# First keys and queries in halves of 256 tokens in lent PSUM banks, with the scheduler's constants fitted anew

## Chip, cores and metric

One core of one Trainium2 chip. The metric is device time in microseconds (us) of that core; lower is better. A time quoted is the median of several executions. Profiles are of one execution each, so a single place in a profile can be off by what one execution differs from the next.

## The reference

One transformer block with layer norm ahead of attention and ahead of a gated feed-forward without a nonlinearity. 2048 tokens, model width 640, 32 heads of 20, feed-forward width 1728, all inputs bf16.

```python
h  = x + softmax(q @ k.T * 20 ** -0.5) @ v @ wo      # q, k, v = layernorm(x) @ wqkv, 32 heads of 20
h2 = h + ((ln(h) @ w_gate) * (ln(h) @ w_up)) @ w_down
```

There are 32 x 2048 x 2048 = 134 million exponentials. They set the pace: ScalarE, which takes 1738 of the 2048 blocks, is busy for 804.5 of the 860.7 us of the profile before the change.

## The kernel before

The kernel contains a scheduler that runs when the kernel is built. It holds an estimate of every instruction's duration, keeps a clock for each engine, and emits the instructions in the order in which its clocks say they would start. So a wrong estimate does no harm to the result, but it puts instructions in a wrong order, and that order is what the chip runs.

Scores are made in *bursts* into PSUM tiles `A` of two or three banks (1024 or 1536 columns). ScalarE takes the exponential of a burst; VectorE makes some blocks itself from banks of `m` or `A`, with integer arithmetic. Then the value product goes into bank `acc`. A *block* is 128 keys by 512 columns of scores; there are 2048 of them. Heads are handled in groups of four, tokens in chunks of 512. All other matmuls (projections, output, gate, up and down) are background *groups*, put in between bursts into the banks `m`. Where TensorE would be idle, *filler* is issued: matmuls on a zero tile `zt`.

```python
# Engines.run: what a transfer is believed to take
if e == "SP":
    self.ring = max(self.ring, s + t.dur) + t.size / 160.0
    slack = SLACK if t.prio > 0 else 300.0            # SLACK = 2000 ns
    t.ev.t = self.ring + 1500.0 + slack

# Pe.fill: what a group of four filler matmuls is believed to take
n = bank.shape[1]
self.charge(s, n / 2.4 + 3.0, self.shape(), float(n), deps, [])

# a background product: four matmuls of 32 columns, or one of 128 once attention is done (mode "F")
def columns(ps, lhsT, rhs, start, stop, n, width=P):
    if pe.mode == "F":
        mm(ps[0:width, 0:n], lhsT[:, 0:width], rhs, start, stop)
        return
    for i in range((width + 31) // 32):
        w = min(32, width - 32 * i)
        mm(ps[32 * i:32 * i + w, 0:n], lhsT[:, 32 * i:32 * i + w], rhs, start, stop)

# the opening: layer norm and transposes of 512 tokens, then keys (1) and queries (0) of two head groups
t0 = stage1_ln(0)
pe.groups += t0
pe.groups += [proj_direct(1, 0, 0, "ACT"), proj_direct(0, 0, 0, "ACT")]
pe.groups += [proj_direct(1, 1, 0, "ACT"), proj_direct(0, 1, 0, "DVE")]
... # cut: further chunks of 512 tokens, values, and the groups due later, with LEAD, LEADQ, LEADK
```

`proj_direct(b, g, ch)` makes five matmul steps over 512 tokens into one bank `m`, which ScalarE or VectorE then evacuates. It needs all four transposed tiles of 128 tokens.

The softmax here doesn't subtract the row's maximum and nothing guards it: scores larger than these inputs give would overflow.

Of the kernel before, what the change touches and what calls it, by code (L numbers as in the profile page):

```python
# [15 lines left out]
P = 128  # L16
# [39 lines left out]
class Ev:  # L56
# [3 lines left out]
    def __init__(self, t=None):  # L60
        self.t, self.slack = t, 0.0


class Max:
# [5 lines left out]
    @property  # L70
    def t(self):
        r = 0.0
        for e in self.es:
            if e.t is None:
                return None
            r = max(r, e.t)
        return r
# [116 lines left out]
class Pe:  # L194
# [78 lines left out]
    def next(self):  # L273
        s, kind, a, latest = self.choose()
        t = self.en.free["PE"]
        if self.att.flat == 0:
            t = max(t, known([self.zeros]))
        if t < INF and (kind == 2 or s > t + 100.0):
            if known([self.zeros]) <= t and (self.att.flat == 0 or sum(w for x, w in self.recent if x > t - TICK) < ENOUGH):
                need = FILL + SWITCH + (SWITCH if self.mode != self.shape() else 0.0)  # L280
                if t + need <= max(latest, s) + 20.0 and t < INF:
                    if self.att.summing() is not None or self.att.between(t) or not self.att.begun or any(b.free.t is not None and b.free.t <= t for b in self.mbanks):
                        return t + 10.0, self.fill
        return s, a

# [38 lines left out]
TICK = 3413.0  # L324
RWEIGHT = 128.0
FILL = 216.0
WINDOW = 30
EBUFS = (3, 5)
NED = 4
NI16 = 3  # L330
SLACK = 2000.0
THIRD = True
AHEAD = 9
VPARTS = [(0, 8), (8, 8), (16, 16)]
OPENS = 4
ENOUGH = 5000.0
SPREAD = (1.0, 1.0, 0.9, 0.8, .8)
LAG0 = 8
LEAD = 64
LEADQ = 64  # L340
LEADK = 16
M_END = 1800
BACK = 14

# [2 lines left out]
def kernel(  # L347
# [31 lines left out]
    def single_banks():  # L379

        if att.flat < att.total or att.a_free[0].t is None or att.a_free[1].t is None or att.third.t is None or len(pools) > 1:
            return
        pools[0].release()
        pools.append(tc.alloc_tile_pool(name="last", bufs=1, space=PSUM))
        for i, t in enumerate(tiles(pools[1], 5, [P, QW], F32, "b")):
            b = Bank(t[:])
            b.free = att.third if i == 2 else att.a_free[0] if i < 2 else att.a_free[1]
            pe.mbanks.append(b)
# [60 lines left out]
    def dve_ns(n, rate=1.0):  # L449
        return n / 0.96 / rate + 70.0  # L450
# [46 lines left out]
    class Att:  # L497
        def __init__(self):
# [47 lines left out]
            self.pending_act = 0.0  # L546
            self.q0 = [sum(WIDTHS[:i]) for i in range(len(WIDTHS))]
            self.kev = {}
            self.qev = {}
            self.vev = {}  # L550

# [93 lines left out]
        def inputs(self, b):  # L645
            s, j = b
            p, g, kg = self.slots[s]
            deps = [self.qev.get((g, p))]
            for k, _, _, _ in pieces(WIDTHS[p], kg):
                deps.append(self.kev.get((g, k // TPC)))  # L650
            return deps if all(d is not None for d in deps) else [Ev()]

        def summing(self):
# [238 lines left out]
    pe = Pe(en, att, filler)  # L892
    en.pe = pe
    def hook():
        single_banks()
        staged()
    en.hook = hook
    pe.mbanks = [Bank(m[:]) for m in mb]

    nn = [0]  # L900
    on_ev = {}
# [284 lines left out]
    def columns_of(b, ch):  # L1186

        return (att.q0[ch], WIDTHS[ch]) if b == 0 else (ch * QW, QW)
# [1 line left out]
    def tokens_ready(o, w):  # L1190
        return [Later(lambda tt=tt: lnT_ev.get(tt)) for tt in range(o // P, (o + w) // P)]

    def proj_direct(b, g, ch, eng="DVE"):
        t0, w = columns_of(b, ch)
        sl = slice(t0, t0 + w)
        o = b * D + g * HP * DH

        def step(c):
            def fn(ps, first, last):
                for j in range(HP):  # L1200
                    mm(ps[32 * j:32 * j + 32, 0:w], Wr[:, c, o + DH * j:o + DH * j + 32], lnT[:, c, sl], first, last)
            return fn

        def evac(ps, e):
            if b == 1:
                if eng == "ACT":
                    r = en.add("ACT", w / 1.2 + 63.0, [e], lambda: nc.scalar.copy(kT[g][:, sl], ps[:, 0:w]), 0)
                else:
                    r = en.add("DVE", dve_ns(w), [e], lambda: nc.vector.tensor_copy(kT[g][:, sl], ps[:, 0:w]), 0.8)
                att.kev[g, ch] = r  # L1210
            else:
                if eng == "ACT":
                    r = en.add("ACT", w / 1.2 + 63.0, [e], lambda: nc.scalar.mul(qT[ch][:, g, :], ps[:, 0:w], kap[:, 0:1]), 0)
                else:
                    r = en.add("DVE", dve_ns(w), [e], lambda: nc.vector.tensor_scalar_mul(qT[ch][:, g, :], ps[:, 0:w], kap[:, 0:1]), 0.8)
                att.qev[g, ch] = r
            return r
        ws = [e_qk0[b]]
        if b == 0:
            ws.append(e_kap)  # L1220
        return Group(tokens_ready(t0, w) + ws, [(pe_ns(w), step(c), []) for c in range(KC)], evac, f"P{b}{g}{ch}")
# [332 lines left out]

    t0 = stage1_ln(0)
    pe.groups += t0
    pe.groups += [proj_direct(1, 0, 0, "ACT"), proj_direct(0, 0, 0, "ACT")]
    pe.groups += [proj_direct(1, 1, 0, "ACT"), proj_direct(0, 1, 0, "DVE")]
    first = pe.groups[-3].ev

# [39 lines left out]

REPORT = []
D_GAP = 0
SHARE = 0.17
D_START = 2 * HP * NT
D_LAST = 40
D_LOAD = 4000.0
D_LOAD0 = 600.0
# [31 lines left out]
```

## Time and profile before

| | before |
|---|---|
| time | 863.93 us, median of 3 (862.95 to 864.56) |
| first exponential | 18.94 us |
| block 1920 of 2048 reaches an engine | 770.12 us |
| last score matmul | 825.61 us |
| end of the profiled execution | 860.67 us |

In this view of stretches each row has its bounds and its length, then the busy time and the number of instructions of TensorE (PE), its weight loads, VectorE, ScalarE (ACT) and GpSimd, the granted TensorE clock, the DMA share, and GB/s. The bounds are: first exponential, third head group (block 128), block 1920, last score, end.

```profile
0.00:18.94 18.94, 16.59 (x317) 8.22 (x317) 10.02 (x35) 4.74 (x7) 6.55 (x20) 1.00 0.81 241
18.94:85.44 66.50, 61.85 (x1365) 28.18 (x1364) 38.34 (x104) 58.91 (x52) 7.38 (x4) 1.00 0.21 57
85.44:770.12 684.68, 656.95 (x12076) 265.16 (x12076) 648.66 (x1321) 682.55 (x636) 6.29 (x7) 1.00 0.25 63
770.12:825.61 55.49, 54.04 (x1720) 34.61 (x1719) 40.08 (x99) 53.06 (x51) 0.69 (x1) 1.00 0.33 73
825.61:860.67 35.06, 31.22 (x381) 24.46 (x378) 17.34 (x49) 5.19 (x16) 0.55 (x1) 0.98 0.05 16
```

In the third row ScalarE is busy for 682.55 of 684.68 us: it is the bound.

### The profile page before, as it was taken

Reading aid. Unit: us, or ns where it says so; the run is one execution under the profiler, and the core shown is the slowest. Engines: PE = TensorE matmul, PEld = TensorE weight load, DVE = VectorE, ACT = ScalarE, POOL = GpSimd, SP = SyncE. Lnnn points to the kernel's source line nnn. Section 1 sums busy time; section 2 is a strip of 40 time slices with the busy share of each in tenths; the row PEclk is TensorE's granted clock in tenths of the full one; section 3 lists DMA queues with packets and bytes.
Section 4 is the critical chain, followed back from the end, with each engine's and each line's share of the span. In section 5 each row is a group of like instructions: output and inputs, shape, how many; then the busy total and the mean of one; then the engine's idle time right before and its main releaser. Section 6 shows DMA issues by size and latency. Waiting matters only on the chain. (4 is left out here: it accounts for less than half of the span.)

```text
span 860.7 us, 35389 instructions
## 1 busy us (share of the span) xinstructions
PE 820.7 (95%) x15853; PEld 360.6 (42%) x15853; DVE 754.4 (88%) x1607; ACT 804.5 (93%) x760; POOL 21.5 (2%) x33
## 2 busy tenths in 40 slices
PE   8899999999989999999989999999999999999998
PEld 4444333223423322223434433344444444556676
DVE  5664889999989999989989999999999999878663
ACT  3889999999999999999999999999999999999941
POOL 3020000000000000000000000000000000000000
PEclk9999999999999999999999999999999999999999
DMA  7221311223324232210310233134024411263200
GB/s 212 65 59 55 99 33 45 86 71 87 97 52 101 57 91 65 54 27 23 87 28 12 54 72 73 35 93 99 16 56 91 107 26 30 50 142 85 47 6 25
DMA packets 131756, 56.25 MB, mean 65 GB/s; under 512 B 102292, under 2 KB 129556, under 8 KB 131604
## 3 DMA queue, kind: packets, MB, share of 16 engines
q1 hardware_dynamic: 131604, 53.99, 24.6%
q8 instruction: 124, 2.03, 1.0%
q14 instruction: 28, 0.23, 0.1%
HBM read 45.63 MB, written 8.09 MB: 62 GB/s over the span
## 5 line engine op out<-in xcount | busy, mean ns | idle before, releaser
L761 ACT ACTIVATE E<-A 128x1536 bf16<-128x1536 f32 (+1 forms) x738 | 795.7, 1218 | 12.7 <-PE A L435 9.0
L435 PE MATMUL A<-qT,kT 32*128 32x256 bf16 (+3 forms) x3009 | 288.9, 297 | 23.9 <-ACT E L761 22.9
L435 PEld LDWEIGHTS <-kT 32*128 32x128 bf16 (+1 forms) x3438 | 94.7, 92 | 247.5 <-issue 130.2
L435 PE MATMUL acc<-E,Vx 128*32 128x256 bf16 (+3 forms) x2828 | 184.8, 302 | 5.8 <-ACT E L761 4.0
L777 DVE TENSOR_SCALAR i<-m 128x512 int16<-128x512 f32 x216 | 147.7, 686 | 15.3 <-PE m L435 13.9
L435 PEld LDWEIGHTS <-Vx 128*32 128x32 bf16 x3328 | 71.1, 95 | 92.8 <-issue 81.8
L809 DVE TENSOR_TENSOR fr<-hl,fr 128x1024 bf16<-128x1024 bf16 x156 | 106.3, 681 | 1.9
L812 DVE TENSOR_TENSOR ED<-i,fr 128x1024 int16<-128x1024 int16 x156 | 106.1, 680 | 1.3
L435 PE MATMUL m<-qT,kT 32*128 32x256 bf16 (+3 forms) x319 | 83.4, 313 | 0.0
L435 PE MATMUL m<-Wd,hh 128*32 128x320 bf16 (+1 forms) x1484 | 75.7, 301 | 0.4 <-DVE ot L1516 0.3
L435 PE MATMUL m<-lnT,Wr 128*32 128x512 bf16 (+6 forms) x1200 | 71.7, 339 | 0.3 <-DVE i L777 0.2
L435 PE MATMUL m<-ln2T,wg 128*32 128x512 bf16 (+2 forms) x1020 | 67.0, 348 | 0.1
L806 DVE TENSOR_SCALAR hl<-fr 128x1024 bf16<-128x1024 int16 x156 | 65.1, 417 | 1.5
L777 DVE TENSOR_SCALAR i<-A 128x512 int16<-128x512 f32 x94 | 64.5, 686 | 1.7 <-PE A L435 1.0
L803 DVE TENSOR_SCALAR fr<-i 128x1024 int16<-128x1024 int16 x156 | 64.4, 419 | 0.9
L435 PE MATMUL m<-ln2T,wu 128*32 128x512 bf16 (+2 forms) x940 | 63.0, 349 | 0.3
L435 PE MATMUL acc<-zt 128*32 128x512 bf16 (+3 forms) x960 | 63.1, 345 | 0.0
L435 PEld LDWEIGHTS <-hh 128*32 128x32 bf16 (+3 forms) x1540 | 42.4, 96 | 27.2 <-issue 15.7
L435 PE MATMUL m<-shared,On 128*32 128x320 bf16 x960 | 46.8, 301 | 0.4 <-DVE shared L1394 0.2
L1493 DVE TENSOR_TENSOR hh<-gs,m 128x512 bf16<-128x512 bf16 (+3 forms) x64 | 34.8, 544 | 8.8 <-PE m L435 7.0
L1482 DVE CAST gs<-m 128x512 bf16<-128x512 f32 (+2 forms) x62 | 34.7, 559 | 8.0 <-PE m L435 7.5
L435 PEld LDWEIGHTS <-zt 128*32 128x32 bf16 x1208 | 29.7, 98 | 26.7 <-issue 13.6
(87 smaller groups left out, 551.5 us busy)
## 6 DMA issues: line engine op xcount, KB each, us to landing
wg<-in_B_w_gate_dram SPq DMA_DIRECT2D x47, 160.0 KB
wu<-in_B_w_up_dram SPq DMA_DIRECT2D x47, 160.0 KB
rb<-rd SPq DMA_DIRECT2D x16, 256.0 KB
kT<-kq SPq DMA_DIRECT2D x24, 128.0 KB
kq<-ln2T SPq DMA_DIRECT2D x24, 120.0 KB
out_dram<-ot SPq DMA_DIRECT2D x16, 160.0 KB
shared<-in_A_x_dram SPq DMA_DIRECT2D x14, 160.0 KB
Wd<-in_B_w_down_dram SPq DMA_DIRECT2D x13, 160.0 KB
```

What stands on the lines that cost most here:

```text
L435: return nc.tensor.matmul(out_, lhsT=lhsT, rhs=rhs, start=start, stop=stop)
L761: r = nc.scalar.activation(E[:, 0:size, :], src[:, 0:size, :], ACT.Exp, scale=LN2_ / UNIT)
L777: r = nc.vector.tensor_scalar(it[:, pos, :], bank.ap, BIAS, 0.0, ALU.add, ALU.max)
L803: nc.vector.tensor_scalar(f[:, 0:n, :], it[:, 0:n, :], 127, None, ALU.bitwise_and)
L806: nc.vector.tensor_scalar(h[:, 0:n, :], f[:, 0:n, :], QR, QK, ALU.subtract, ALU.mult)
L809: nc.vector.tensor_tensor(fb[:, 0:n, :], h[:, 0:n, :], f[:, 0:n, :], ALU.mult)
L812: nc.vector.tensor_tensor(e16[:, 0:n, :], it[:, 0:n, :], fb[:, 0:n, :], ALU.add)
L1482: r = en.add("DVE", dve_ns(w), [e, was], lambda: nc.vector.tensor_copy(gs[0:M, 0:w], ps[0:M, 0:w]), 1)
L1493: r = en.add("DVE", dve_ns(w), [e, ce, was], lambda: nc.vector.tensor_tensor(hh[0:M, 0:w], gs[0:M, 0:w], ps[0:M, 0:w], ALU.mult), 1)
```

## The change

The intent: make the first scores sooner. The first keys and queries are projected in halves of 256 tokens, so that the first halves can be made while the third and fourth tiles are still being transposed. The extra banks for that are lent: `acc` and one bank of `A` serve as background banks until the first score. Around that, the constants of the scheduler were fitted anew.

```diff
-WINDOW = 30
+WINDOW = 20
-AHEAD = 9
+AHEAD = 7
-SPREAD = (1.0, 1.0, 0.9, 0.8, .8)
-LAG0 = 8
-LEAD = 64
-LEADQ = 64
-LEADK = 16
+SPREAD = (1.2, 1.2, 1.0, 1.0, 1.0)
+LAG0 = 4
+LEAD = 56
+LEADQ = 80
+LEADK = 8
-SHARE = 0.17
-D_START = 2 * HP * NT
+SHARE = 0.18
+D_START = 112
     def hook():
+        if att.flat > 0:
+            while lent:
+                pe.mbanks.remove(lent.pop())
+    lent = [Bank(acc[:]), Bank(A[1][:, 0, :])]
+    pe.mbanks += lent
+    att.acc_free, att.a_free[1] = Free(lent[0]), Free(lent[1])
-    pe.groups += [proj_direct(1, 0, 0, "ACT"), proj_direct(0, 0, 0, "ACT")]
+    pe.groups[2:2] = [proj_direct(1, 0, 0, "ACT", 0), proj_direct(0, 0, 0, "ACT", 0)]
+    pe.groups += [proj_direct(0, 0, 0, "ACT", 1), proj_direct(1, 0, 0, "DVE", 1)]
... # cut: proj_direct's argument half (which 256 tokens), an event for each key tile in place of one for the chunk,
    # class Free (passes on when a lent bank is free), and a clause dropped from the condition for filler before the first score
```

LEAD, LEADQ and LEADK say how many blocks ahead of their use projections are due; SPREAD how the feed-forward groups are spread; SHARE and D_START what share of the blocks goes to VectorE and from which block.

More of the change, by code (lines that the diff above doesn't have):

```diff
@@ L281, in next @@
                 if t + need <= max(latest, s) + 20.0 and t < INF:
-                    if self.att.summing() is not None or self.att.between(t) or not self.att.begun or any(b.free.t is not None and b.free.t <= t for b in self.mbanks):
+                    if self.att.summing() is not None or self.att.between(t) or any(b.free.t is not None and b.free.t <= t for b in self.mbanks):
                         return t + 10.0, self.fill
@@ L548, in __init__ @@
             self.kev = {}
+            self.kev_tile = {}
             self.qev = {}
@@ L649, in inputs @@
             for k, _, _, _ in pieces(WIDTHS[p], kg):
-                deps.append(self.kev.get((g, k // TPC)))
+                deps.append(self.kev_tile.get((g, k)) or self.kev.get((g, k // TPC)))
             return deps if all(d is not None for d in deps) else [Ev()]
@@ L898, with __init__, t @@
     pe.mbanks = [Bank(m[:]) for m in mb]
+    class Free:
+        __slots__ = ("bank",)
+        def __init__(self, bank):
+            self.bank = bank
+        @property
+        def t(self):
+            return self.bank.free.t
+    lent = [Bank(acc[:]), Bank(A[1][:, 0, :])]
+    pe.mbanks += lent
+    att.acc_free, att.a_free[1] = Free(lent[0]), Free(lent[1])
     nn = [0]
@@ L1191, in tokens_ready, with proj_direct @@
         return [Later(lambda tt=tt: lnT_ev.get(tt)) for tt in range(o // P, (o + w) // P)]
-    def proj_direct(b, g, ch, eng="DVE"):
+    halves = {}
+    def proj_direct(b, g, ch, eng="DVE", half=None):
         t0, w = columns_of(b, ch)
+        if half is not None:
+            w //= 2
+            t0 += half * w
         sl = slice(t0, t0 + w)
+        qsl = slice(0, w) if half is None else sl
         o = b * D + g * HP * DH
@@ L1209, in evac @@
                     r = en.add("DVE", dve_ns(w), [e], lambda: nc.vector.tensor_copy(kT[g][:, sl], ps[:, 0:w]), 0.8)
-                att.kev[g, ch] = r
             else:
                 if eng == "ACT":
-                    r = en.add("ACT", w / 1.2 + 63.0, [e], lambda: nc.scalar.mul(qT[ch][:, g, :], ps[:, 0:w], kap[:, 0:1]), 0)
+                    r = en.add("ACT", w / 1.2 + 63.0, [e], lambda: nc.scalar.mul(qT[ch][:, g, qsl], ps[:, 0:w], kap[:, 0:1]), 0)
                 else:
-                    r = en.add("DVE", dve_ns(w), [e], lambda: nc.vector.tensor_scalar_mul(qT[ch][:, g, :], ps[:, 0:w], kap[:, 0:1]), 0.8)
-                att.qev[g, ch] = r
+                    r = en.add("DVE", dve_ns(w), [e], lambda: nc.vector.tensor_scalar_mul(qT[ch][:, g, qsl], ps[:, 0:w], kap[:, 0:1]), 0.8)
+            done = r
+            if half is not None:
+                halves[b, half] = r
+                if b == 1:
+                    for k in range(t0 // P, (t0 + w) // P):
+                        att.kev_tile[g, k] = r
+                done = Max(list(halves[b, i] for i in range(2))) if (b, 1 - half) in halves else None
+            if done is not None:
+                (att.kev if b == 1 else att.qev)[g, ch] = done
             return r
```

## The prediction

> **What bounds the kernel now.** I read the page first, for which engine has no slack, then that engine's own timeline, then TensorE beside it wherever it stalls.
>
> ```profile
> PE 820.7 (95%) x15853; PEld 360.6 (42%) x15853; DVE 754.4 (88%) x1607; ACT 804.5 (93%) x760; POOL 21.5 (2%) x33
> L761 ACT ACTIVATE E<-A 128x1536 bf16<-128x1536 f32 (+1 forms) x738 | 795.7, 1218 | 12.7 <-PE A L435 9.0
> L435 PE MATMUL acc<-zt 128*32 128x512 bf16 (+3 forms) x960 | 63.1, 345 | 0.0
> ```
>
> TensorE shows 95%, but some of that is filler: matmuls on a zero tile (zt), at least 63 us of it[...]. ScalarE has no filler. It does 738 exponentials, 795.7 us of them, with only 12.7 us idle before them. So the span is three pieces laid end to end: until the first exponential, the stream of exponentials, and what remains after the last. Next, ScalarE's timeline at the start:
>
> ```profile
> 16.67 0.59 ACT L1207 CAST kT<-m 128x512 bf16<-128x512 f32 x1 [2.35 <-PE m L435]
> 17.75 0.69 ACT L1213 ACTIVATE qT<-m,kap 128x512 bf16<-128x512 f32 x1 [0.49 <-PE m L435]
> 18.94 1.45 ACT L761 ACTIVATE E<-A 128x1536 bf16<-128x1536 f32 x1 [0.51 <-PE A L435]
> 20.29 0.58 ACT L1207 CAST kT<-m 128x512 bf16<-128x512 f32 x1
> 20.75 12.34 ACT L761 ACTIVATE E<-A 128x1024 bf16<-128x1024 f32 x11
> 35.39 15.20 ACT L761 ACTIVATE E<-A 128x1536 bf16<-128x1536 f32 x13 [2.29 <-PE A L435]
> 54.41 7.80 ACT L761 ACTIVATE E<-A 128x1024 bf16<-128x1024 f32 x7 [3.83 <-PE A L435]
> ```
>
> The first exponential starts at 18.94 us. The stream stalls for 2.29 us when it needs the keys of tokens 512 to 1023, and for 3.83 us when it needs the next 512; a third stall, 1.35 us at 85.4, comes where the third group of heads begins (block 128 of 2048). The last exponential ends at 827.1. The tail is 33.6 us, and TensorE fills it:
>
> ```profile
> 825.43 0.39 PE L435 MATMUL A<-qT,kT 32*128 32x128 bf16 x4
> 830.45 0.71 PE L435 MATMUL m<-ln2T,kT 128*128 128x256 bf16 x5
> 831.00 0.71 PE L435 MATMUL b<-ln2T,kT 128*128 128x256 bf16 x5
> 836.45 2.17 PE L435 MATMUL b<-Wd,hh 128*128 128x320 bf16 x14
> ```
>
> The last score matmul starts at 825.43, the end is at 860.7. In between are gate and up groups of five matmuls, 0.55 us apart (830.45 to 831.00), then the down projections. The chain of waits for the end has almost only TensorE in it, so work taken out of this tail is time saved.
>
> [...] means of 1490 and 1069 ns, start to start mostly 1330 and 904 ns; I use the trace's. [...] 109 ns for 256 columns, which is the 0.55 us for five above.
>
> **The change, part by part.** I compared the built orders of both kernels' instructions: they carry no times, but exact counts.
>
> *1. The first scores.* Before, the projections wait for the fourth transposed tile: VectorE copies it by 15.29, TensorE starts at 15.35 on 512 tokens of keys, then 512 of queries, ScalarE evacuates one after the other (16.67, 17.75), scores at 18.50. After, the first half of keys (acc) and of queries (m) are made while the third and fourth tiles are still being transposed; one transpose borrows a bank of A. Filler before the first transpose is unchanged (132 matmuls in both orders), so the transposes still start at 11.05. Behind the fourth tile's copy at about 15.2 there is left: the second query half (5 x 0.108 us + 0.28 us latency = 0.82), its evacuation (about 0.48: the 0.69 us of 512 columns less 256 x 0.82 ns, the slope between the 1490 and 1069 ns above), 0.4 for scores and hand-overs. ScalarE's queue also holds a key half and the third tile's copy before them, which costs some tenths. First exponential at about 17.4: **-1.5 us**.
>
> *2. The two chunk stalls.* In the new order the third tile group is normalised, transposed and projected with the key projection right after burst 12 of the scores, and with fewer copies before VectorE's key copy. Laying the new order out with the trace's durations from 17.4 on: burst 12 at about 29.2, key projection 29.5 to 30.9, copy to 31.6, burst 13 exponentiated at about 32.0, against 35.39. The stream would be ready at about 31.2, so a stall of about 0.8 remains: **another -1.9 us** (3.4 ahead in all). For the next chunk the limit is VectorE: its statistics now stand behind the second group's partial sum, its copies of transposed tiles come before the following chunk's normalisation instead of between, but 1.5 us of that normalisation stands before the key copy. I get burst 26 at 50.2 against 54.41, a stall of about 3.4: **another -0.8 us** (4.2 ahead).
>
> *3. The step to the third group.* Between its last burst on the second group and its first on the third, TensorE had 20 projection matmuls of 512 columns, 56 value matmuls of 160 and 8 of the sum (82.22 to 85.02, 2.8 us). The new order has 36, 100 and 8. With about 0.054 us and 0.02 us each: 16 x 0.054 + 44 x 0.02 = **+1.75 us** of added stall there. About 2.4 us ahead remains.
>
> *4. The stream.* The share constant goes from 0.17 to 0.18 and the start from 128 to 112, which sounds like work moving from ScalarE to VectorE. It doesn't: both orders give VectorE 310 of 2048 blocks and ScalarE 1738; the other limits (load, pending pairs) bind. What changes is their cut: 474 two-bank and 263 three-bank exponentials become 495 and 249. 21 x 0.904 - 14 x 1.334 = **+0.3 us**.
>
> *5. The tail.* Counted after the last score matmul, 55 gate/up matmuls of 256 columns on the full array become 30: five groups of 0.55 = 2.7 us. Some eight quarter-width ones (0.25) and 16 of the sum (0.2) go as well: **-3.2 us**. Those groups haven't vanished: they run before the last score, in the last 128 blocks, where the order holds 35.4 us of non-filler column time against 34.2, and where TensorE has next to no filler to give up (1.1 us before, 0.6 after). ScalarE already lost 4.9 us of that stretch to late scores (starts later than 1.33 or 0.90 us after the one before, summed). I charge **+1.2 us**.
>
> *6. Spreading.* Later starts for the feed-forward groups move work out of blocks 640 to 1023 (filler there rises from 8.9 to 15.2 us) into 1024 to 1791 (falls from 13.1 to 4.7). ScalarE lost about 1 us per 128 blocks there before whatever the load, 1.4 in the fullest stretch (33.3 us non-filler). The new fullest is 32.8. I charge +0.3.
>
> Sum: -1.5 - 1.9 - 0.8 + 1.75 + 0.3 - 3.2 + 1.2 + 0.3 = -3.85. With a little credit because the constants were fitted to this order: **859.5 us**, 0.5% less than 863.93.
>
> **Rivals.** (a) The head start is swallowed: if the later chunks' transfers or the DRAM round trip of the third group's keys arrive at fixed times, the stream only waits longer at 85 us, and just the tail counts: about 861. For it: the query read of that group now stands in the transfer queue behind the copy-out of the first group's sums. Against it: the two chunk stalls follow instruction order, with their data long landed, and that copy-out moves earlier too. (b) TensorE becomes the bound: with 8.4 us less filler in the second half, modelled times that are too short (320-column groups above all) make bursts late, 0.5 to 1 us per 128 blocks over six stretches; then the gain is gone, 862 to 865. For it: the 4.9 us lost in the last stretch. Against: bursts have priority, and a stretch with 33.3 lost only 1.4. (c) Everything lands: both chunk stalls nearly vanish (5 us), the third group is no later, tail in full: 853 to 855. For 2% the span would have to lose 17.3 us, more than all start stalls (7.5) and the tail's change together.
>
> **Range and chances.** Terms 1 and 5 I trust within 0.7 us; 2, 3 and 6 rest on an order laid out by hand and can each be off by 2. Together that is about 3.5 us one way, some more for rival (b): 853.5 to 864. Faster by over 2%: 0.03; within: 0.96; slower by over 2%: 0.01.
>
> **What would show it.** First exponential near 17.4. The stall of the 13th below 1 us, that of the 25th or 26th still 2 to 4. A stall of about 3 us at 80 to 83. 744 or 745 exponentials. From last score to end near 32.0 instead of 35.2. In the middle no stretch of 128 blocks losing over 1.5 us. I am wrong if the third group starts at 85 us or later although the first started early (a), if ScalarE's loss between 425 and 720 us grows by over 2 us (b), or if the last score comes so late that the tail's gain is given back in full.

(That no bank was to be had beyond the kernel's own, 1 of `acc`, 2 of `m`, 2 + 3 of `A`, was not shown. The durations are in the trace of the kernel before. The means of 1490 and 1069 ns are those of exponentials of 1536 and 1024 columns. A group of four 32-wide matmuls of 512 columns starts 216 ns after the one before it: 0.054 us each, and 0.108 for a group of 256 columns. Full-width matmuls of 256 columns start 109 ns apart, and one alone takes 273 ns, its 0.28. 24 value matmuls of 160 columns take 0.54 us (84.48 to 85.02), 0.02 each. "Column time" is the count of columns at 2.4 per ns, the scheduler's price; 512 in 216 ns is 2.37.)

## The result, and the profile after

The changed kernel took 861.26 us, median of 4 (861.18 to 862.05); the kernel before, in the same rounds, 863.50 us (4 runs). The ratio is 0.9975, with a 95% interval of 0.9957 to 0.9992: the same within 2%, and 2.2 us less. Ratios are computed as the mean time of one kernel's fast runs over that of the other's of the same rounds, so they are not quite the ratio of the medians. Other rounds gave 861.01 against 863.43 us (ratio 0.9973).

The page of the changed kernel:

```profile
PE 820.1 (95%) x15808; PEld 356.9 (42%) x15808; DVE 751.9 (88%) x1604; ACT 804.5 (94%) x768; POOL 21.8 (3%) x33
L762 ACT ACTIVATE E<-A 128x1536 bf16<-128x1536 f32 (+2 forms) x745 | 795.8, 1211 | 16.0 <-PE A L435 13.3
L435 PE MATMUL acc<-zt 128*32 128x512 bf16 (+3 forms) x852 | 62.5, 359 | 0.0
```

745 exponentials, as the built order had said. ScalarE's idle time before them rose from 12.7 to 16.0 us. ScalarE's timeline of the opening:

```profile
17.34 2.36 ACT L762 ACTIVATE E<-A 128x1536 bf16<-128x1536 f32 x2 [0.49 <-PE A L435]
...
29.86 2.37 ACT L762 ACTIVATE E<-A 128x1024 bf16<-128x1024 f32 x2 [0.63 <-PE A L435]
32.81 15.10 ACT L762 ACTIVATE E<-A 128x1536 bf16<-128x1536 f32 x13 [0.58 <-PE A L435]
51.62 29.66 ACT L762 ACTIVATE E<-A 128x1024 bf16<-128x1024 f32 x26 [3.71 <-PE A L435]
84.64 16.41 ACT L762 ACTIVATE E<-A 128x1024 bf16<-128x1024 f32 x15 [3.36 <-PE A L435]
```

The first exponential is 1.6 us sooner, the 13th 2.6, the 26th 2.8, the third group 0.8. So the opening works, and the step to the third group (the last line, a stop of 3.36 us against 1.35) takes most of it. The stretches, bounded as before:

```profile
17.34:84.64 67.30, 64.46 (x1439) 29.43 (x1432) 43.92 (x121) 59.02 (x53) 7.39 (x4) 1.00 0.22 60
84.64:768.32 683.68, 655.36 (x11900) 260.43 (x11902) 644.98 (x1318) 681.52 (x642) 6.63 (x7) 1.00 0.25 63
768.32:828.01 59.69, 56.75 (x1823) 36.98 (x1812) 40.66 (x99) 54.98 (x53) 0.70 (x1) 0.97 0.35 70
828.01:859.25 31.24, 27.98 (x332) 21.59 (x329) 15.32 (x44) 4.31 (x15) 0.56 (x1) 1.00 0.05 18
```

Block 1920 is reached 1.80 us sooner (768.32 against 770.12). The tail is 3.82 us shorter (31.24 against 35.06), more than predicted. But the stretch before it is 4.20 us longer (59.69 against 55.49). Stretch and tail together, the tail's gain is more than gone: 90.93 against 90.55.

Of the 59.69 us TensorE is idle for 2.94; before it was 1.45 of 55.49. The view of waits for this stretch names what ended TensorE's idle times (us in total, times, longest us):

```profile
PE A L435 <- issue: 1.8, 2, 1.3
PE acc L435 <- issue: 0.7, 1, 0.7
PE m L435 <- issue: 0.3, 1, 0.3
PE A L435 <- ACT E L762: 0.2, 1, 0.2
```

TensorE's timeline at the largest stop:

```profile
812.40 0.50 PE L435 MATMUL m<-ln2T,qT 128*32 128x256 bf16 x12
812.84 0.22 PE L435 MATMUL A<-qT,kT 32*128 32x128 bf16 x1
814.37 0.40 PE L435 MATMUL A<-qT,kT 32*128 32x128 bf16 x11 [1.31 <-issue]
```

A burst of twelve score matmuls is cut after the first, and "issue" says that no semaphore or engine that the profile shows held it. What was under way then was a transfer of instructions. Here is the view of the DMA queues between 810.35 and 814.40 us:

```profile
q1 hardware_dynamic: 264, 0.07, 8.2%
q8 instruction: 1, 0.02, 4.2%
```

There is one packet on the queue named instruction, 16 KB. 4.2% of 16 engines over 4.05 us is 2.7 us for it; the trace has it from 810.38 to 813.12. TensorE took about 174 further instructions (matmuls and weight loads) after that transfer began, stopped at 813.06, and went on 1.25 us after the landing. The median of such transfers is 1.0 to 1.1 us in every profile.

How many instructions come with one such transfer can be counted. The queue has 123 packets of 16,384 bytes each, 2.02 MB in all. From the start of the first to the start of the last TensorE took 31,143 matmuls and weight loads, 255 for each; in the kernel before it is 254 (31,299). The stops that end at 798.02 and 814.37 us are 1,024 instructions apart, four times 256. So my estimate is one transfer for each 256 of TensorE's instructions. For most of the run no stop follows one: between 20 us and block 1920 neither profile has a stop of TensorE without a releaser over 0.15 us. In this stretch there are four (0.49, 0.65, 1.31 and 0.30 us). An estimate from the trace's numbers: at 61 instructions per us (3635 in 59.69 us) 174 instructions last 2.8 us. A normal transfer needs 1.0 us and some 1.25 us after landing, 2.3 us in all, and fits. A slow one of 1.9 us or more doesn't. (This turned out too simple: see "Why the prediction was right or wrong".) In the long middle, at 35 per us, the same 174 last 5 us.

So my theory going into the experiments, not yet shown: the extra length of the last stretch is partly work that was moved there, as I had predicted, but mostly TensorE's stops for instructions, whose place follows from where the 256-instruction boundaries fall. The rival: the stretch is long because of the work, and the stops only take slack. A second question was which part of the change brought the gain.

### The profile page after: what moved, and what is told of

Same layout as the page of the kernel before. It is cut to its first block, busy times and chain, and to the rows that moved or that the text cites. A ratio compares the mean times of both kernels' runs of the same rounds, so it can differ in the third digit from the quotient of the medians.

```text
span 859.3 us, 35305 instructions
## 1 busy us (share of the span) xinstructions
PE 820.1 (95%) x15808; PEld 356.9 (42%) x15808; DVE 751.9 (88%) x1604; ACT 804.5 (94%) x768; POOL 21.8 (3%) x33
## 3 DMA queue, kind: packets, MB, share of 16 engines
q8 instruction: 123, 2.02, 1.0%
## 4 chain that ended last, share of the span: by engine, by line
ACT 63%; PE 28%; issue 5%; DVE 4%; POOL 0%; ACTq 0%; POOLq 0%
ACT E L762 63%; PE m L435 13%; PE A L435 7%; PE acc L435 5%; PE b L435 2%; DVE i L778 1%; DVE fr L810 1%; DVE ED L813 1%; DVE hl L807 0%; DVE fr L804 0%; PE m L1071 0%; DVE gs L1515 0%; DVE hh L1526 0%; DVE accS L955 0%; DVE Vx L1325 0%
## 5 line engine op out<-in xcount | busy, mean ns | idle before, releaser
L762 ACT ACTIVATE E<-A 128x1536 bf16<-128x1536 f32 (+2 forms) x745 | 795.8, 1211 | 16.0 <-PE A L435 13.3
L435 PE MATMUL A<-qT,kT 32*128 32x256 bf16 (+3 forms) x3037 | 292.2, 297 | 25.6 <-ACT E L762 20.9
L435 PEld LDWEIGHTS <-kT 32*128 32x128 bf16 (+2 forms) x3513 | 95.2, 92 | 258.3 <-issue 138.2
L778 DVE TENSOR_SCALAR i<-m 128x512 int16<-128x512 f32 x200 | 136.1, 684 | 11.4 <-PE m L435 9.7
L778 DVE TENSOR_SCALAR i<-A 128x512 int16<-128x512 f32 x110 | 75.2, 684 | 8.8 <-PE A L435 7.9
L435 PE MATMUL m<-qT,kT 32*128 32x256 bf16 (+3 forms) x291 | 77.1, 314 | 0.0
L435 PE MATMUL m<-lnT,Wr 128*32 128x512 bf16 (+7 forms) x1180 | 69.8, 336 | 0.4
L435 PE MATMUL m<-shared,On 128*32 128x320 bf16 (+1 forms) x968 | 47.5, 301 | 0.4 <-DVE i L778 0.3
L435 PEld LDWEIGHTS <-Wr 128*32 128x32 bf16 x1240 | 27.3, 95 | 24.2 <-issue 15.3
```

The lines of the kernel that those rows point to most:

```text
L435: return nc.tensor.matmul(out_, lhsT=lhsT, rhs=rhs, start=start, stop=stop)
L762: r = nc.scalar.activation(E[:, 0:size, :], src[:, 0:size, :], ACT.Exp, scale=LN2_ / UNIT)
L778: r = nc.vector.tensor_scalar(it[:, pos, :], bank.ap, BIAS, 0.0, ALU.add, ALU.max)
```

## The experiments

Eleven runs followed, one of them the changed kernel again, all correct, each with five rounds beside the kernel before. "Stretch" is block 1920 to the last score, "tail" the last score to the end, "idle" TensorE's time without a matmul in the stretch, all from one profile each.

| kernel | us, median | lowest to highest | ratio | block 1920 | stretch | idle in it | tail |
|---|---|---|---|---|---|---|---|
| before (first profile) | 863.4 | 861.7 to 864.7 | 1 | 770.12 | 55.49 | 1.45 | 35.06 |
| changed (first profile) | 861.26 | 861.18 to 862.05 | 0.9975 | 768.32 | 59.69 | 2.94 | 31.24 |
| e7_again (changed, again) | 861.01 | 859.56 to 861.67 | 0.9973 | 767.86 | 59.53 | 4.10 | 31.23 |
| e1_halves | 868.68 | 866.02 to 872.10 | 1.0066 | 770.12 | 56.58 | 3.88 | 37.32 |
| e2_consts | 859.58 | 858.68 to 861.21 | 0.9958 | 769.57 | 52.06 | 1.09 | 36.07 |
| e3_spread | 861.14 | 860.30 to 863.23 | 0.9980 | 766.65 | 56.76 | 2.50 | 35.56 |
| e4_cold | 858.13 | 857.55 to 858.94 | 0.9941 | 767.67 | 56.70 | 1.69 | 31.23 |
| e5_wide | 859.96 | 859.61 to 860.04 | 0.9962 | 768.16 | 58.20 | 0.59 | 31.33 |
| e6_phase | 861.67 | 860.24 to 863.35 | 0.9982 | 768.11 | 58.55 | 2.53 | 31.54 |
| c2_consts_cold | 858.90 | 856.82 to 862.20 | 0.9954 | 767.17 | 52.91 | 1.82 | 36.05 |
| e8_slack | 860.69 | 860.11 to 861.82 | 0.9975 | 765.71 | 55.66 | 1.49 | 36.69 |
| c1_cold_only | 860.81 | 860.11 to 862.07 | 0.9981 | 768.72 | 54.42 | 0.54 | 35.07 |
| c3_cold_slack | 859.14 | 858.21 to 859.45 | 0.9955 | 764.25 | 56.12 | 2.69 | 36.69 |

The times of three sets of rounds stand in it; the kernel before had medians of 863.38, 863.43 and 863.16 in them, so they can be compared within some tenths.

### e1_halves: the halves alone

The changed kernel with all nine constants set back:

```diff
-WINDOW = 20; AHEAD = 7; SPREAD = (1.2, 1.2, 1.0, 1.0, 1.0); LAG0 = 4
+WINDOW = 30; AHEAD = 9; SPREAD = (1.0, 1.0, 0.9, 0.8, .8); LAG0 = 8
-LEAD = 56; LEADQ = 80; LEADK = 8; SHARE = 0.18; D_START = 112
+LEAD = 64; LEADQ = 64; LEADK = 16; SHARE = 0.17; D_START = 2 * HP * NT
```

> The halves and the lent banks alone, all constants as before. Both theories: first exponential near 17.3 us as in the changed kernel. Theory A (the head start is mostly swallowed where the third head group begins): this order has 116 value matmuls, 40 projection matmuls and 12 fillers before the third group's first scores, against 100, 36 and 0 in the changed kernel, so the third group starts near 85.5 us and the time is that of the kernel before within 1 us (862.5 to 864.5). Rival B (the halves carry the gain of the change): 860.5 to 861.5 us.

Measured: 868.68 us, 5.3 us slower than before. The first exponential came at 17.12 us, as early as in the full change. ScalarE's timeline at the third group:

```profile
88.17 11.94 ACT L762 ACTIVATE E<-A 128x1024 bf16<-128x1024 f32 x11 [4.98 <-PE A L435]
```

That is 2.7 us later than before the change. At block 1920 it is level with the kernel before (770.12 in both), and stretch and tail take 93.9 us against 90.6, with 3.9 us of TensorE idle in the stretch. So the halves without the constants lose everything and more; neither theory had that. The profiled execution was the fastest of the six (866.02 us), so the profile shows 3.3 of the 5.3 us.

### e2_consts: the constants alone

The kernel before with the new constants, the same nine the other way round.

> The new constants alone, projections whole and no lent banks. First exponential near 18.9 us. The order gives VectorE 317 blocks instead of 310, so ScalarE's stream is some 2.2 us shorter (243 three-bank and 501 two-bank exponentials). Theory A (each part is worth about 1 to 2 us, and the scheduler re-deals the rest): 861 to 863 us. Rival B (the constants only serve the halves): 863.5 us or more.

Measured: 859.58 us, 1.7 us *faster* than the full change. The first exponential is at 17.92 us, the third group at 86.59 (a stop of 2.06 us), block 1920 at 769.57. That is 1.25 us behind the full change at this point, but stretch and tail take 88.1 us against 90.9. The time lies below both of my ranges: the constants bring the gain by themselves. My credit in the prediction "because the constants were fitted to this order" was wrong: they suit the old opening at least as well.

Two things in this profile I had overlooked. It has an early window of half clock, in which the 13th to 26th exponentials lose 1.45 us against c2_consts_cold (20.48 us in place of 19.03); without it, I estimate block 1920 at about 768.1, as soon as in the full change:

```profile
38.63:42.04 3.41, 3.41 (x30) 0.76 (x22) 3.41 (x15) 2.51 (x3) 1.01 (x1) 0.50 0.02 5
```

And TensorE's work in stretch and tail is that of the full change (busy for 83.3 us; 83.4 in e7_again). The difference is idle time, 4.8 us against 7.35. So part of what the constants seem to bring may be where the stops fall. Which constant does it, apart from SPREAD below, no run tells.

### e3_spread: one constant

```diff
-SPREAD = (1.2, 1.2, 1.0, 1.0, 1.0)
+SPREAD = (1.0, 1.0, 0.9, 0.8, .8)
```

> The changed kernel with the old spread of the feed-forward groups alone. The order is the same up to about block 640; after the last score 29.3 us of column time are left instead of 25.3, in the last 128 blocks 33.3 instead of 35.4. Theory A (TensorE is full in the last stretch and after it, so work moved across the last score changes nothing): the time from last score to end grows by about 4 us, the last score comes about 4 us earlier, and the total stays within 1 us of 861.3. Rival B (the shorter tail is a real gain, and the last stretch was held up by something else, such as the stalls of TensorE with no releaser, 1.31 us the longest): about 864 us.

Measured: 861.14 us, the same as the full change, as Theory A had it. With the old SPREAD block 1920 comes 1.7 us sooner, and stretch and tail take 1.4 us longer: one for the other.

### e4_cold: the opening's filler at its real price

The starts of the filler in the trace of the kernel before are 427 ns apart for the first ten groups of four, then 216 ns. In the thirteen profiles the first 6 to 12 groups were slow in this way, at twice the time, and full speed came 2.6 to 5.4 us after the first matmul. I call it the slow clock of the start. (The granted clock in the view of stretches shows 1.00 for the opening all the same.) The scheduler prices every group at 216 ns, so it puts too many ahead of the first transpose:

```diff
-        self.charge(s, n / 2.4 + 3.0, self.shape(), float(n), deps, [])
+        self.charge(s, n / (1.2 if s < 4200.0 else 2.4) + 3.0, self.shape(), float(n), deps, [])
```

> The changed kernel, but the scheduler prices fillers before 4.2 us of its own clock at half the TensorE clock, as the trace shows them (9.5 us for 33 groups of four, not 7.1). The order is the same but for 100 instead of 132 fillers before the first transpose. Theory A (the opening is bound by the fillers ahead of the first transpose, and all that follows shifts with it): first transpose near 9.7 instead of 11.45 us, first exponential near 15.6, total 859.5. Rival B (something later, a transfer or the layer norm of the third and fourth tile, holds the opening or the third group): first exponential or third group no earlier, total 861.3.

TensorE's opening, in the changed kernel:

```profile
1.73 9.90 PE L435 MATMUL m<-zt 128*32 128x512 bf16 x132 [1.73 <-POOL zt L1142]
11.45 0.73 PE L1071 MATMUL m<-ident,shared 128*32 128x128 bf16 x40
```

And in e4_cold, where 32 filler matmuls are gone and a stop with no releaser has come in:

```profile
1.72 8.02 PE L435 MATMUL m<-zt 128*32 128x512 bf16 x100 [1.72 <-POOL zt L1142]
9.58 0.72 PE L1071 MATMUL m<-ident,shared 128*32 128x128 bf16 x40
...
13.68 0.22 PE L1071 MATMUL m<-ident,shared 128*32 128x128 bf16 x1 [0.92 <-issue]
```

Measured: 858.13 us, the best of all, 3.1 us less than the changed kernel. The first exponential came at 16.63 us (15.6 expected). But the opening isn't where most of it came from. At block 1920 it is 0.2 to 0.65 us ahead of the two profiles of the changed kernel. From there on both kernels have the same instructions in the same order: 1823 or 1824 matmuls and 1812 weight loads in the stretch, 332 and 329 in the tail. Yet e4_cold takes 56.70 us for the stretch:

```profile
767.67:824.37 56.70, 55.01 (x1824) 36.35 (x1812) 40.80 (x100) 54.49 (x53) 0.70 (x1) 1.00 0.37 74
824.37:855.60 31.23, 27.98 (x332) 21.59 (x329) 15.23 (x44) 4.61 (x16) 0.55 (x1) 1.00 0.05 18
```

Against 59.69 and 59.53 us, with the tail the same to 0.01 us. The second profile of the changed kernel (e7_again, below) has this row for the stretch:

```profile
767.86:827.39 59.53, 55.43 (x1824) 36.23 (x1812) 40.64 (x99) 54.83 (x53) 0.70 (x1) 1.00 0.35 70
```

The idle time went from 2.94 and 4.10 to 1.69 us. What differs is the phase: 32 matmuls fewer in the opening, each with its weight load, shift every later instruction by 64 against the blocks of 256. This spoke for the fetches.

### e7_again: the changed kernel once more

> The changed kernel itself once more, for a second profile and a tighter ratio in the same rounds as the others. If the stops of 2.75 us in the last stretch belong to this order and phase of instructions, they come again at the same instructions with 2 to 3 us in sum and the time is 861.0 to 862; if they are chance of one execution, the sum is under 1.5 us or falls at other instructions, and single times scatter by over 1.5 us. The window of half TensorE clock at 816 to 820 us: comes again if it follows from the stop of 1.3 us before it.

Measured: 861.01 us. TensorE's timeline at the same place as above:

```profile
813.31 0.22 PE L435 MATMUL A<-qT,kT 32*128 32x128 bf16 x1
814.84 0.40 PE L435 MATMUL A<-qT,kT 32*128 32x128 bf16 x11 [1.31 <-issue]
```

The stop is there again, after the same first matmul of the same burst, again 1.31 us, after an instruction transfer that took 2.64 us. So it belongs to this order and this phase. Others moved: a new one of 1.08 us at 806.25, and the one at 798 us grew from 0.49 to 1.04. The sum, 3.7 us in the list of stops, is above what I expected; the scatter of the times, 2.1 us, too.

The other question was the clock. After the stop, the changed kernel's first profile had TensorE at half clock for 3.41 us, from 815.98, 1.6 us after the stop ended. First its stretch from 816 to 820 us, then, in the second fence, e7_again's:

```profile
816.00:820.00 4.00, 4.00 (x96) 2.64 (x92) 1.05 (x3) 3.22 (x4) 0.00 (x0) 0.58 0.07 16
```

```profile
816.00:820.00 4.00, 3.90 (x129) 2.70 (x126) 1.56 (x6) 4.00 (x4) 0.00 (x0) 1.00 0.06 16
```

Granted clock 0.58 with 96 matmuls in the one, 1.00 with 129 in the other. By estimate the half clock costs up to 1.7 us when it comes (half of 3.41), but it doesn't follow from the stop every time.

### e5_wide: fewer instructions for the same work

The direct test: from block 1920 on, background products are emitted as one matmul 128 columns wide in place of four of 32. (The expectation calls them value products. What the edit touches is the background products: gate, up, down and output projection. The value products stay narrow.)

```diff
-        if pe.mode == "F":
+        if pe.mode == "F" or att.flat >= 1920:
             mm(ps[0:width, 0:n], lhsT[:, 0:width], rhs, start, stop)
```

> The changed kernel with one edit: from query block 1920 on, the value products of a step are emitted as one matmul 128 columns wide in place of four 32 wide, over the same data in the same order; nothing else moves and TensorE's column time is the same, but the last stretch has about a quarter as many instructions of that kind. Instruction-fetch theory: the stops of TensorE in the middle of a burst that have no releaser (2.75 us in the profiled run of the changed kernel after 797 us, each just after a 16 KB instruction transfer that took over 1.9 us) go to under 0.5 us in the last stretch, because TensorE no longer uses up its instructions faster than they come; the last stretch shrinks from 59.7 to about 56.5 to 57.5 us, and the time is 857.5 to 859.5 us. Rival (the stretch is long because more column work of TensorE was left to it, and the stops are a by-product): the stops may go but the end stays at 860.5 to 862. [...]

(The expectation puts every stop of the first profile after a transfer of over 1.9 us. That is a misreading: only the one of 1.31 us follows such a transfer; the other three follow transfers of 0.88, 1.52 and 1.63 us.)

Measured: 859.96 us, 1.05 us less than the changed kernel of the same rounds. TensorE's timeline at the place of the stop:

```profile
813.31 0.50 PE L435 MATMUL m<-ln2T,qT 128*128 128x256 bf16 x3
813.74 0.40 PE L435 MATMUL A<-qT,kT 32*128 32x128 bf16 x12
814.08 0.39 PE L435 MATMUL m<-ln2T,qT 128*128 128x256 bf16 x2
```

Twelve score matmuls in one go. The list of stops in the whole stretch has one left, 0.46 us, and the slowest instruction transfer took 1.62 us. The stretch:

```profile
768.16:826.36 58.20, 57.61 (x1296) 34.50 (x1288) 40.99 (x100) 55.04 (x53) 0.69 (x1) 1.00 0.35 72
```

1296 matmuls in place of 1824, and idle down from 4.10 (e7_again) to 0.59 us. But the busy time rose from 55.4 to 57.6 us, so only 1.3 of 3.5 us came through. My expectations of 56.5 to 57.5 us for the stretch and of 857.5 to 859.5 us for the time missed; the time is also below the range of the rival. What the wide form costs can be read from the traces. In e7_again the background products and the value products have the same shape, 128*32, and where a background product follows a value product it starts 58 ns after it on average. In e5_wide the background products have 128*128, and in that place, 20 times in the stretch, they start 155 ns after it. That makes 1.9 of the 2.2 us by which the busy time rose. The spacing of value products among themselves is as before.

One more thing stands in the times: five executions within 0.43 us (859.61 to 860.04). The other kernels of the table, apart from the changed kernel's first four, scatter over 1.2 to 6.1. That fewer stops make the time steadier isn't shown: c1_cold_only has no stop in its stretch and scatters over 2.0.

### e6_phase: the phase alone

16 filler groups between blocks 640 and 1023 aren't emitted; the scheduler's clocks and so the order are as before.

```diff
+        if 640 <= self.att.flat < 1024 and self.skipped < 16 and not new:
+            self.skipped += 1
+            return
         self.filler(bank, new)
```

> The changed kernel with 16 groups of filler matmuls (64 to 128 instructions that compute nothing used) not emitted somewhere between blocks 640 and 1023; the order of everything else is the same, and only the places at which the 256-instruction transfers end move. Instruction-fetch theory: the start of block 1920 stays within 0.5 us of 768.3, but the stops without a releaser in the last stretch fall in other places and sum to something else than 2.75 us, and the time moves by 0.5 to 3 us, in either direction (down more likely, since the changed kernel's sum is the second largest seen). Rival (same order, same end): 861.3 within 0.4 us, and stops of 2.4 to 3 us again. [...]

Measured: 861.67 us (860.24 to 863.35), within the rival's 0.4 us. Block 1920 is at 768.11, as expected. But the stops did move: the place at 814 us has none, and a new one of 1.60 us cuts a value product in two at another place of the same order, 1.31 us after the landing of an instruction transfer that took 2.87 us, and again with a window of half clock after it:

```profile
823.01 0.35 PE L439 MATMUL acc<-E,Vx 128*32 128x128 bf16 x11 [1.60 <-issue]
```

So the phase decides where the stops fall; that they would sum to another time in the median, it didn't show. But the median says little here: the six executions form two groups, 860.2 to 860.7 and 862.6 to 863.4 us, and it lies between them. The profile is of the first group; the second has a lower mean granted clock (0.996 to 0.998, against 0.998 to 1.000). So this run decides neither for the theory nor for the rival. Of the two shifts of phase that ran, the one by 64 instructions (e4_cold) gave 3 us, and the one by 128 (this one) no clear gain.

### c1_cold_only and c2_consts_cold: the old opening with the filler priced right

The line of e4_cold put into the kernel before, and into e2_consts.

> The kernel before, no halves and none of the new constants, with the filler of the opening priced at its slow clock (100 in place of 132 filler matmuls ahead of the first transpose, all else in the same order). Theory: the first transpose at about 9.0 in place of 11.05 us, the first exponential at 17.2 to 18.0 in place of 18.94, so that most of what the halves were made for can be had by a price; the steps ahead of blocks 13, 26 and 128 swallow part, 862.2 to 863.0 us against 863.4. Rival (nothing before block 128 reaches the end of the old order): 863.4 within 0.4; other places of the instruction transfers may move it by up to 1.5 us either way.

Measured: 860.81 us, better than I expected. ScalarE's first exponential, without any halves:

```profile
17.51 1.45 ACT L761 ACTIVATE E<-A 128x1536 bf16<-128x1536 f32 x1 [0.51 <-PE A L435]
```

17.51 us, against 17.34 for the changed kernel, and that although TensorE lost 1.49 us to a stop with no releaser at 13.74 us on the way. Of the 2.5 us that the profile is shorter (858.21 against 860.67), 1.40 are there at block 1920, and 1.07 came in the stretch, whose order is that of the kernel before: its idle time fell from 1.45 to 0.54 us. Tail 35.07 against 35.06.

> The kernel before with the new constants alone (859.6 us) and, besides, the filler of the opening priced at the slow clock that it really has (100 filler matmuls ahead of the first transpose in place of 132; the rest of the order as with the constants alone). Theory: the first transpose comes 1.5 to 1.9 us sooner and the first exponential at about 16.3 in place of 17.9, as with the changed kernel (11.45 to 9.58 us there, and 0.8 us sooner to the first exponential with a fetch stop in it); of that 0.6 to 1.5 us reach the end: 858.1 to 859.0 us. Rival (head start swallowed by the steps at blocks 13, 26 and 128): 859.6 within 0.4. If instruction fetches fall badly in the last stretch, up to 861.

Measured: 858.90 us (856.82 to 862.20). In the profile block 1920 is 2.40 us sooner than in e2_consts, more than the first exponential (16.99 against 17.92); the other 1.45 us are the window of half clock in e2_consts. A stop of 1.06 us fell into the stretch, and single times scatter over 5.4 us. It isn't told apart from e4_cold (858.13).

### e8_slack and c3_cold_slack: the step to the third group

The third group's keys and queries are written to DRAM and read back. (The expectation calls them weights.) In the changed kernel its queries had landed by 80.27 us (the expectation says 79.8), but its scores started at 84.21. In between stand other matmuls, because the scheduler believed in a later landing. TensorE's timeline in the changed kernel:

```profile
81.82 0.88 PE L435 MATMUL m<-Wr,lnT 128*32 128x160 bf16 x40
82.88 0.53 PE L435 MATMUL m<-Wr,lnT 128*32 128x160 bf16 x20 [0.18 <-DVE Vx L1325]
83.22 1.05 PE L435 MATMUL m<-lnT,Wr 128*32 128x512 bf16 x16
84.21 0.39 PE L435 MATMUL A<-qT,kT 32*128 32x512 bf16 x2
```

The edit shortens the allowance for that group's transfers alone:

```diff
-                slack = SLACK if t.prio > 0 else 300.0
+                slack = 300.0 if t.prio <= 0 else 500.0 if t.size == 3 * P * QW * 2 and self.pe.att.flat <= 128 else SLACK
```

> The changed kernel with the weights of the third head group alone believed to land 500 ns after the estimate in place of the long allowance of the changed kernel; the order then puts 20 in place of 36 half-width query/key products between the last scores of the second group and the first of the third. Theory (the third group was late because the scheduler, not the transfer, put other TensorE work first; the query weights had landed at 79.8 us and TensorE came to those scores only at 84.2): the stop of ScalarE of 3.36 us ahead of the third group falls below 1.5 us and the group starts at 82.0 to 83.0 in place of 84.4 to 84.6. What of it reaches the end: block 1920 starts 0 to 1.5 us sooner; the tail is 2 to 4 us longer and the last stretch 2 to 4 shorter, since its order is another, so 859.5 to 861.5 us. Rival (the transfer is the wait): the group starts at 84.4 again, with a DMA named as the releaser.

Measured: 860.69 us. The 16 products at 83.22 are gone from before the scores:

```profile
83.16 0.53 PE L435 MATMUL m<-Wr,lnT 128*32 128x160 bf16 x20 [0.18 <-DVE Vx L1325]
83.62 0.39 PE L435 MATMUL A<-qT,kT 32*128 32x512 bf16 x2
```

ScalarE's stop fell from 3.36 to 2.50 us, not below 1.5, and the group started at 84.05: this execution's opening was late (first exponential 17.61). From the 26th exponential to the group it is 32.16 us against 33.02. The 0.86 us are the 16 matmuls at 0.054 us. No DMA is named as releaser, so the rival fell: it is TensorE's order. The 100 value projections (56 before the change) stand there still, which is why so much of the stop stays. And block 1920 came 2.2 to 2.6 us sooner, though not by the head start alone, since in this order VectorE makes 314 blocks in place of 310; but stretch and tail took 92.35 us in place of 90.8 or 90.9: two thirds of it is given back.

> The changed kernel with both, the opening's filler at its real price (858.1 us alone) and the third group's weights believed sooner. If the gains add: third group at 81.5 to 82.5 us, 856.5 to 858.0 us. If the third group's lead is swallowed later because TensorE is the bound of the last stretch whatever the start: 858 to 859. If the new order falls on bad instruction transfers: up to 860.

Measured: 859.14 us. The third group started at 82.57, block 1920 came at 764.25, 3.4 us before e4_cold, and stretch and tail took 92.8 us against 87.9. The gains don't add; this one came out 1.0 us behind e4_cold alone. The order built with this edit has more of TensorE's work at the end: it is busy for 86.9 us in stretch and tail, against 83.0 in e4_cold. An earlier stream alone doesn't do that: c1_cold_only, with the order of the kernel before, keeps its 1.4 us up to block 1920 and loses none of it behind.

## Why the prediction was right or wrong

The class was right, and the time lies inside the range. The point of 859.5 us was 1.8 us too low: the change brought 2.2 to 2.4 us of the 3.85, or of 4.4 with the credit.

**Term 1, the first scores (-1.5).** Right: 17.34 us against a predicted 17.4. But it is less sharp than it looks: over the six profiles with this opening the first exponential lay between 16.60 and 17.61 us, and the first transpose between 10.47 and 11.51, because the slow clock of the start lasts longer in one execution than in another (6 to 12 groups of filler at 427 ns). From the first transpose to the first exponential it is 5.89 us against 7.89 before; in the 7.89 falls a stop of TensorE with no releaser of 0.62 us (at 14.25) which the prediction carried over into its 15.2 us. So the agreement within 0.1 us is partly luck.

**Term 2, the chunk stalls (-1.9 and -0.8).** Right in kind, too large. The 13th exponential stalled for 0.58 us as predicted (below 1), the 26th for 3.71 (2 to 4). But the lead was 2.6 and 2.8 us in place of 3.4 and 4.2. My layout by hand had missed a small stop of 0.63 us at 29.86; the rest of the difference I haven't traced.

**Term 3, the third group (+1.75).** Close: the lead fell by 2.0 us, from 2.8 to 0.8, with the predicted stop of about 3 us (3.36). Why it was so is now shown: TensorE's order, not the transfer (e8_slack).

**Terms 4 and 6 (+0.3 each).** Both too pessimistic: between the third group and block 1920 the kernel gained 1.0 us. 0.5 of it is the cut: in this part 20 two-bank exponentials more and 14 three-bank ones less, 20 x 0.904 - 14 x 1.330, as VectorE took one block more. ScalarE's time lost to late scores there was 14.8 us against 15.2, so the spreading cost nothing, and rival (b) fell for the middle. At block 1920 the lead was 1.80 us; the sum of my terms to that point was 1.85. The errors had cancelled.

**Term 5, the tail (-3.2) and the last 128 blocks (+1.2).** This is the step that failed: in the prediction's words, "I charge +1.2 us". The tail gained 3.8 us. The last 128 blocks lost 4.2 us, and 4.0 in the second profile. The +1.2 was a fair size for the work that moved: at full clock TensorE was busy there for 55.0 us (e4_cold) and 55.4 us (e7_again) against 54.04 before. What it left out is TensorE's stops without a releaser: its idle time there rose by 1.5 us in one profile and 2.65 in the other, and the list of stops without a releaser there rose from 0.9 to 2.8 and 3.7 us, and in the first profile up to 1.7 us of half clock came on top. With that, my own condition for being wrong was met: the last score came so late (828.01 against 825.61) that the tail's gain was given back in full.

Three runs carry this: e4_cold has the same instructions in the same order from block 1920 and is 3 us faster over them; e5_wide has the same work in fewer instructions, and all stops but one of 0.46 us go; e7_again has the stop at the same matmul a second time. What e5_wide also shows is that the stops are worth less than their sum when they are removed at the price of changes of shape.

The traces hold a stronger sign, which I had overlooked. Count TensorE's matmuls and weight loads from the first. In the 13 profiles 45 stops without a releaser last over 0.15 us. The count at the end of each leaves a remainder of 183 to 191 when divided by 256. So they fall, within a few instructions, at places that are multiples of 256 apart, about as many instructions as come with one transfer (254 and 255 by the counts above), and nowhere else. All lie before 20 us or after block 1920, and each of the 38 over 0.25 us ends 1.0 to 1.6 us after an instruction transfer has landed.

A slow transfer isn't the only cause, though. Before the stops at, for example, 802.04 us (changed kernel), 806.25 (e7_again) and 793.03 (c3_cold_slack) the transfer took 0.9 us, but it began late: TensorE took only 71 to 119 instructions from its start to the stop. Over all stops it is 71 to about 200, mostly 155 to 185. And c1_cold_only had two transfers of 2.0 and 2.2 us without a stop: 1.25 us after their landing TensorE had taken 175 and 180 instructions since they began, about as many as ahead of most stops.

**The rivals.** Rival (a) named 861, which is what came, but for another reason. It had the head start swallowed by fixed arrival times at the third group and only the tail count. In truth 1.8 us of head start reached block 1920, and the tail's gain is what was swallowed. Rival (b), TensorE as the bound, was right in the last stretch alone, and there not through misjudged durations.

**What stays open.** Why some instruction transfers take 1.9 to 2.9 us, and why others begin late. In the 13 profiles 60 of the 62 that took over 1.5 us overlapped another transfer, while 505 of all 1593 overlapped none; but many that overlapped one were quick, and no run tested it. Why the half clock follows one such stop and not another, and comes in e2_consts after idle times of 0.45 and 0.96 us. And how much of the difference between kernels within 1 us is only the phase of their instruction blocks: e4_cold, c2_consts_cold, c3_cold_slack and e2_consts aren't told apart for sure.

Both kernels are beaten by e4_cold: 858.13 us, ratio 0.9941 (0.9929 to 0.9953), one changed line away from the changed kernel.

## What to carry to other kernels

When work is moved ahead of the last score, look at what bounds the stretch that it moves into: here TensorE was busy for 97% of it, so what left the tail came back. Many narrow matmuls also use up instructions (61 per us in the last stretch here, 35 in the long middle): where a stop falls inside a burst and nothing released it, count the instructions per microsecond and look at the transfers of instructions before you look for a semaphore. And check constants that were fitted along with a change on the old kernel too, and the prices of the opening: here the constants alone, and a single price alone, each did at least as much as the whole change.
